# Routing attention and feed-forward on one core: clusters chosen through VectorE's 32x32 block transposes, softmax sums taken over two halves, centroids loaded first

## The chip, the core and the metric

The kernel runs on one core of a Trainium2 chip. The core has a matrix engine (TensorE, PE in the profile; its weight loads are listed as PEld), a vector engine (VectorE, DVE), a scalar engine (ScalarE, ACT), GpSimd (POOL) and SyncE (SP), which issues most of the DMA transfers. The engines run side by side and wait for one another through semaphores. TensorE writes its results to a small memory called PSUM; everything else lies in SBUF. The metric is the time of one execution on the device, in microseconds (us).

## What is computed

Two stages follow each other. The first is attention in which a query sees only the keys of its own cluster; the second is a two-layer feed-forward block with a layer norm ahead of it and a residual.

```python
# q, k, v: 4 batches x 8 heads x 768 tokens x 64, float32; 16 centroids per head
q_assign = argmax(einsum('bhsd,hcd->bhsc', q_n, c_n))    # rows normalised
k_assign = argmax(einsum('bhsd,hcd->bhsc', k_n, c_n))
scores = scale * q @ k^T, and -1e9 where q_assign != k_assign
attn = exp(scores - max) / (sum(exp(scores - max)) + 1e-9)
x = attn @ v                                             # heads side by side: 4 x 768 x 512
xn = (x - mean) / sqrt(var + 1e-6) * g_ln
out = x + relu(xn @ w_ch1) @ w_ch2                       # 512 -> 2048 -> 512
```

The length of a query or key doesn't change which centroid is nearest, so the kernel normalises only the centroids.

## The kernel before

**Tiling.** Two heads make a pair; 4 batches of 4 pairs give 16 pairs, numbered n. The 768 tokens are six tiles of 128 (`NT`), or two halves of 384 (`HC`, index g). For a pair, q and k lie transposed in SBUF (`t0`, `t1`): the 64 features of the first head (j = 0) in partitions 0 to 63, of the second in 64 to 127. A score tile has 128 keys as partitions and 384 queries as columns, one for each head.

**The loop.** The order of PE, DVE and ACT is written out by hand. Each pair has two slots, one for each half g of the queries. In a slot TensorE computes six score tiles for each head (`scores`), some smaller products, and then weighs the values with the exponentials (`weigh`, 24 matmul records). Each score tile is the sum of two products: one of bfloat16 mask tiles, which adds a huge negative number where the clusters differ, and one of k and q. ScalarE then takes the exponential (L391) into `e`. Score tiles have three buffers, so that TensorE can be a few ahead of ScalarE. After the weighing ScalarE copies the result to `x` (L422).

**Choosing clusters for pair n+1 while pair n is at work.** In slot 0 `prep_transpose` turns k and q on VectorE (L278) and `prep_sims` multiplies them with the centroids (L300). Its result has four groups of 32 rows: queries and keys of the first half, queries and keys of the second; in each, 16 clusters of one head and 16 of the other. ScalarE copies it to SBUF (L309), `prep_turn` transposes it on TensorE in three pieces (L316), after the weighing of slot 0, and `prep_route` lets VectorE find the greatest of each 16 (L325) and mark it with a one (L327). In slot 1, between the scores and the weighing, `prep_onehot` transposes the marks back on TensorE in six pieces (L342), and ScalarE writes the masks in three instructions (L363): `m` over all 128 partitions, and two strips of 16 partitions of `mask`. For the first pair the strips are written by VectorE (L365).

**Softmax sums.** VectorE adds the six exponential tiles of a half (`add_up`): L439 and L442 add them in twos, leaving two partial sums side by side, and L444 adds these to one tile, `es`. In slot 0 of the next pair `finish(n, 0)` multiplies `es` with a matrix of ones (L456, four matmuls, each into a strip of 32 partitions of one bank), and ScalarE copies the sums out (L464). The bank is shared with `weigh`, which has to wait for that copy. The last pair adds its tiles one after another (L432).

**Start.** `load(0, "q")`, the centroids and `load(0, "k")` are issued on SP in this order (half of q and k on ACT). `norm_centroids` normalises the centroids on VectorE with one square root on ScalarE, `turn_centroids` transposes them, and `busy` runs filler matmuls. The first pair's q and k are transposed on TensorE (L283). VectorE also converts the feed-forward weights in the loop (L246 to L266). The feed-forward stage, from about 339 us on, isn't touched.

Of the kernel before, what the change touches and what calls it, by code (L numbers as in the profile page):

```python
# [19 lines left out]
def kernel(  # L20
# [94 lines left out]
                    )  # L115
            loaded[n][name] = t

    load(0, "q")

    c_sb = const.tile([H * NCL, D], F32, name="c_sb")  # L120
    nc.sync.dma_start(out=c_sb, in_=centroids.rearrange("h c d -> (h c) d"))
    load(0, "k")

    ident = const.tile([P, P], F32, name="ident")
    make_identity(nc, ident)
    identb = const.tile([P, P], BF16, name="identb")
    nc.gpsimd.tensor_copy(identb, ident)
# [12 lines left out]
    onehot = route.tile([P, TH, NHALF, 2, 2, Q], BF16, name="onehot")  # L140
    nc.gpsimd.memset(onehot, 0.0)
    NG = TH * NHALF * 2 * 2

    mask = heads.tile([P, S], BF16, name="mask", bufs=1)
    nc.gpsimd.memset(mask, 0.0)
    hits = const.tile([P, B * NPAIR], F32, name="hits")
    far = const.tile([P, 2], F32, name="far")
    for rows, bias, scale in ((slice(0, D), 0.0, 1.0), (slice(D, P), -FAR, FAR)):  # L150
        nc.gpsimd.memset(far[rows, 0:1], bias)
        nc.gpsimd.memset(far[rows, 1:2], scale)

    DE = HC // Q
    rdens = const.tile([P, B * NPAIR, DE], F32, name="rdens")
# [137 lines left out]
    def prep_sims(n):  # L293

        _, pr = pairs[n]
        sim = ps("sim_ps")
        for side in range(2):
            for g in range(NHALF):
                r = (g * 2 + side) * Q
                nc.tensor.matmul(  # L300
                    sim[r : r + Q, :HC],
                    cT[:, pr, :, :].rearrange("p j c -> p (j c)"),
                    prepared[n][side][:, g * HC : (g + 1) * HC],
                    start=True,
                    stop=True,
                    tile_position=(0, r),
                )
        sim_sb = route.tile([P, HC], F32, tag="sim", name="sim_sb")
        nc.scalar.copy(sim_sb, sim[:, :HC])  # L309
        prepared[n]["sim"] = sim_sb  # L310

    def prep_turn(n):
        sim_sb = prepared[n]["sim"]
        simT = ps("simT_ps")
        for c in range(TH):
            nc.tensor.transpose(  # L316
                simT[:, c * P : (c + 1) * P], sim_sb[:, c * P : (c + 1) * P], ident
            )
        prepared[n]["simT"] = simT

    def prep_route(n):
        simT = prepared[n]["simT"]
        sims = simT[:, :HC].rearrange("p (g c) -> p g c", c=NCL)
        best = route.tile([P, NG], F32, tag="best", name="best")
        nc.vector.tensor_reduce(best, sims, AX.X, ALU.max)  # L325

        nc.vector.scalar_tensor_tensor(  # L327
            out=onehot.rearrange("p c g s j d -> p (c g s j) d")[:, :, :NCL],
            in0=sims,
            scalar=1.0,  # L330
            in1=best.unsqueeze(2).to_broadcast([P, NG, NCL]),
            op0=ALU.mult,
            op1=ALU.is_equal,
            accum_out=hits[:, n : n + 1],
        )

    def prep_onehot(n):
        t = ps("oh_ps", BF16, 1024)
        for g in range(NHALF):
            for c in range(TH):  # L340
                o = (g * TH + c) * P
                nc.tensor.transpose(  # L342
                    t[:, o : o + P],
                    onehot[:, c, g, :, :, :].rearrange("p s j d -> p (s j d)"),
                    identb,
                )

        m = heads.tile([P, S], BF16, tag="m", name="m", bufs=1)
        shade(n, m, t[:, :S], slice(0, P))
        z = mask  # L350
        prepared[n]["oh"] = t
        prepared[n]["m"] = [(z[:D], m[:D]), (m[D:], z[D:])]

    def prep_mask(n, j):
        t, z = prepared[n]["oh"], mask
        src, dst = ((D, 0), (Q, D + Q))[j]
        src, dst = slice(src, src + NCL), slice(dst, dst + NCL)
        shade(n, z[dst], t[src, :S], src)

    def shade(n, out, src, rows):  # L360
        add, factor = far[rows, 0:1], far[rows, 1:2]
        if n or rows == slice(0, P):
            nc.scalar.activation(out, src, AF.Identity, bias=add, scale=factor)  # L363
        else:
            nc.vector.tensor_scalar(out, src, factor, add, op0=ALU.mult, op1=ALU.add)  # L365

# [11 lines left out]
    def scores(i, first="mask", parts=("mask", "qk", "exp")):  # L378
        n, g, c = steps[i]
        st = prepared[n]  # L380
        if parts[0] == first:
            st["s", i] = ps_s.tile([P, 2, 512], F32, tag="s", name="s_ps")
        s = st["s", i]
        keys, cols = slice(c * P, (c + 1) * P), slice(g * HC, (g + 1) * HC)
        rows = [slice(j * D, (j + 1) * D) for j in range(2)]
        for part in parts:
            if part == "exp":
                if c % 2 == 0:
                    soft[i // 2] = attn.tile([P, 2, 2, HC], F32, tag="e", name="e", bufs=4)
                e = soft[i // 2][:, c % 2]  # L390
                nc.scalar.activation(e, s[:, :, :HC], AF.Exp, scale=SCALE)  # L391
                continue
            for j in range(2):
                of_keys, of_queries = st["m"][j] if part == "mask" else [st[i][rows[j]] for i in (1, 0)]
                nc.tensor.matmul(  # L395
                    s[:, j, :HC], of_keys[:, keys], of_queries[:, cols],
                    start=part == first, stop=part != first, skip_group_check=True,
                )

# [25 lines left out]
    def add_up(n, g, parts=range(2)):  # L425
        u = (n * NHALF + g) * NT // 2
        if n + 1 == len(pairs):

            es = xpool.tile([P, 2, HC], F32, tag="row", name="es", bufs=2)
            e = [two[:, h] for two in [soft.pop(u + m) for m in range(NT // 2)] for h in range(2)]  # L430
            for m in range(1, NT):
                nc.vector.tensor_tensor(es, e[0] if m == 1 else es, e[m], ALU.add)  # L432
            sums[n, g] = es
            return
        if 0 in parts:
            two = xpool.tile([P, 3, S], F32, tag="sums", name="two", bufs=2)
            two = two[:, :2].rearrange("p h (j c) -> p h j c", j=2)
            sums[n, g] = two
            nc.vector.tensor_tensor(two, soft.pop(u), soft.pop(u + 1), ALU.add)  # L439
        if 1 in parts:  # L440
            two = sums[n, g]
            nc.vector.tensor_tensor(two, two, soft.pop(u + 2), ALU.add)  # L442
            es = last.tile([P, 2, HC], F32, tag="es", name="es", bufs=3)
            nc.vector.tensor_tensor(es, two[:, 0], two[:, 1], ALU.add)  # L444
            sums[n, g] = es

    def finish(n, part):
        b, pr = pairs[n]  # L450
        if part == 0:
            den = ps_a.tile([P, 512], F32, tag="a", name="den_ps") if n + 1 < len(pairs) else ps("den_ps")
            for j in range(2):
                for g in range(NHALF):
                    r = (j * NHALF + g) * Q
                    nc.tensor.matmul(  # L456
                        den[r : r + Q, :HC], ones, sums[n, g][:, j, :],
                        start=True, stop=True, tile_position=(0, r),
                    )
# [178 lines left out]
    for n in range(len(pairs) - 1):  # L638
        for slot in (0, 1) if n < TWICE else (0,):
            convert[n, slot] = len(convert)  # L640
    order = {mybir.EngineType.PE, mybir.EngineType.DVE, mybir.EngineType.Activation}
    limit[0] = len(convert)
    with tc.manual_schedule(engines=order | {mybir.EngineType.SP}):
# [6 lines left out]

        busy(26)
        norm_centroids(0)
        prep_transpose(0, 0)
        load(1, "q")
        load(0, "v")
        norm_centroids(1)
        norm_centroids(2)
        busy(4)
        prep_transpose(0, 1)
        load(1, "k")  # L660
        busy(8)
        turn_centroids()
        busy(8)
        nc.scalar.activation(warm, warm, AF.Exp, scale=0.0)
        prep_sims(0)
        busy(10)
        prep_turn(0)
        scores(0, "qk", ("qk",))
        prep_route(0)
        prep_onehot(0)  # L670
        prep_mask(0, 0)
        prep_mask(0, 1)
        for i in range(1, AHEAD):
            scores(i, "qk", ("qk",))
        for i in range(AHEAD):
            scores(i, "qk", ("mask", "exp"))
# [2 lines left out]
    with tc.manual_schedule(engines=order | {mybir.EngineType.Pool}):  # L679
        for u in range(len(pairs) * slots):  # L680
# [12 lines left out]
            if slot == 0:  # L693
                if n and nxt:
                    finish(n - 1, 0)
                if nxt:
                    prep_sims(n + 1)
            elif nxt:
                prep_onehot(n + 1)
                prep_mask(n + 1, 0)  # L700
                prep_mask(n + 1, 1)
            for job in extra.pop((n, f"between {slot}"), ()):
                job()
            if slot and n > 1 and nxt:
# [15 lines left out]
            if slot == 0:  # L720
                load(n + 1, "v")
                if nxt:
                    prep_turn(n + 1)
                    prep_route(n + 1)
                else:
                    for part in (2, 3):
# [479 lines left out]
```

## Time and profile before

Three runs took 925.67, 925.93 and 926.99 us; the median is 925.93.

| | |
|---|---|
| profiled execution | 926.89 us |
| span of its instructions | 925.0 us |
| until the first weighing starts | 19.4 us |
| the attention loop, to the first feed-forward matmul | 319.2 us |
| feed-forward | 586.4 us |
| busy in the loop: PE, DVE, ACT | 317.5, 292.4, 225.1 us |

The profile lists groups of instructions by line, engine, operation and tiles: how often, the busy time in all, the mean length of one in nanoseconds, and the idle time of the engine just ahead of them with what ended it. Records of TensorE overlap, since matmuls are pipelined: a record's length is not what it adds to the time, and the distance from one start to the next is read from the timeline.

```profile
L316 PE MATMUL simT_ps<-ident,sim_sb 128*128 128x128 f32 x48 | 8.7, 291 | 0.0
L342 PE MATMUL oh_ps<-identb,onehot 128*128 128x128 bf16 x96 | 8.1, 221 | 0.4 <-DVE onehot L327 0.4
...
L444 DVE TENSOR_TENSOR es<-two 128x768 f32<-128x768 f32 x30 | 28.7, 958 | 1.0
```

"128x128 f32" is the shape of the moving operand, x48 the count of records, "8.7, 291" the busy microseconds of the group and the mean nanoseconds of one record.

### The profile page before, as it was taken

What the parts mean: (1) busy time and instruction counts of PE and PEld (TensorE: products, weight loads), DVE (VectorE), ACT (ScalarE), POOL (GpSimd) and SP (SyncE); (2) the same over time, 40 slices, a digit from 0 to 9 for tenths busy, and PEclk for the clock granted to TensorE, in tenths of its full rate; (3) what the DMA queues carried; (4) which work ended last, traced back from release to release, by engine and by line L of the source; (5) the groups of instructions that cost most, each with busy time, mean ns of one, the idle gap of its engine ahead of it and who ended that gap; (6) DMA issues with size and microseconds to landing.
All of it is one profiled execution on the core that took longest, in us unless ns stands there. A gap on an engine that the chain in (4) does not pass through costs nothing.

```text
span 925.0 us, 12294 instructions
## 1 busy us (share of the span) xinstructions
PE 913.7 (99%) x4634; PEld 584.9 (63%) x4634; DVE 610.4 (66%) x1050; ACT 346.1 (37%) x545; POOL 77.7 (8%) x145
## 2 busy tenths in 40 slices
PE   8999999999999999999999999999999999999997
PEld 4444444444444445568885558886557887557886
DVE  5989999998899879989763446362446372435331
ACT  4677677668777743330003330002331001332000
POOL 1112222111112111110000000000000000000000
PEclk9999999999999999999999999999999999999999
DMA  7778889998796346645530002120002021000011
GB/s 161 145 167 164 162 166 193 212 189 172 164 197 134 83 90 162 141 114 167 164 105 6 0 1 97 54 75 14 0 1 86 29 92 34 1 1 11 26 46 37
DMA packets 186578, 89.32 MB, mean 97 GB/s; under 512 B 153632, under 2 KB 170128, under 8 KB 186512
## 3 DMA queue, kind: packets, MB, share of 16 engines
q1 hardware_dynamic: 177200, 73.09, 33.5%
q0 software_dynamic: 7712, 14.99, 8.2%
q8 instruction: 38, 0.62, 0.3%
q10 hardware_dynamic: 1600, 0.39, 0.2%
q14 instruction: 28, 0.23, 0.1%
HBM read 62.52 MB, written 17.52 MB: 87 GB/s over the span
## 4 chain that ended last, share of the span: by engine, by line
PE 98%; ACT 0%; DMA 0%; DVE 0%; issue 0%; SPq 0%; ACTq 0%; DVEq 0%
PE x_ps L867 18%; PE x_ps L774 18%; PE s_ps L395 17%; PE a_ps L407 14%; PE z_ps L867 9%; PE z_ps L774 9%; PE y_ps L867 4%; PE y_ps L774 4%; PE den_ps L456 1%; PE sim_ps L300 1%; PE simT_ps L316 1%; PE oh_ps L342 1%; DMA k_sb<-in_k_dram 0%; ACT e L391 0%; DVE mask L365 0%
## 5 line engine op out<-in xcount | busy, mean ns | idle before, releaser
L391 ACT ACTIVATE e<-s_ps 128x768 f32<-128x768 f32 x192 | 152.5, 812 | 23.2 <-PE s_ps L395 20.2
L395 PE MATMUL s_ps<-t,t 64*128 64x384 f32 x768 | 155.1, 483 | 0.0
L407 PE MATMUL a_ps<-e,v_sb 128*64 128x384 f32 x768 | 130.9, 490 | 0.0
L407 PEld LDWEIGHTS a_ps<-e,v_sb 128*64 128x64 f32 x768 | 52.3, 137 | 69.6 <-issue 58.3
L794 DVE TENSOR_TENSOR h<-z_ps,u 128x384 f32<-128x384 f32 x64 | 35.6, 556 | 91.2 <-PE z_ps L774 68.7
L395 PEld LDWEIGHTS s_ps<-t,t 64*128 64x128 f32 x768 | 68.1, 188 | 35.0 <-issue 34.4
L867 PE MATMUL x_ps<-w2t,h 128*128 128x256 f32 x384 | 84.5, 379 | 0.0
L802 ACT ACTIVATE h<-h 128x384 f32<-128x384 f32 x96 | 49.5, 522 | 85.6 <-DVE h L794 85.6
L867 PEld LDWEIGHTS x_ps<-w2t,h 128*128 128x128 f32 x384 | 72.7, 190 | 10.1
L395 PE MATMUL s_ps<-m,mask 64*128 64x384 bf16 x192 | 62.1, 324 | 1.6 <-ACT e L391 1.2
L395 PE MATMUL s_ps<-mask,m 64*128 64x384 bf16 x192 | 61.9, 324 | 0.4 <-DVE mask L365 0.4
L439 DVE TENSOR_TENSOR two<-e 128x1536 f32<-128x1536 f32 x30 | 52.6, 1753 | 11.7 <-ACT e L391 11.7
L789 ACT COPY u<-x_ps 128x384 f32<-128x384 f32 x64 | 30.6, 479 | 75.1 <-PE x_ps L774 75.1
L442 DVE TENSOR_TENSOR two<-two,e 128x1536 f32<-128x1536 f32 x30 | 52.6, 1754 | 1.7
L878 DVE TENSOR_TENSOR o_sb<-x_ps,xb 128x256 f32<-128x256 f32 x48 | 20.1, 418 | 49.1 <-PE x_ps L867 49.1
L789 ACT COPY p<-x_ps 128x384 f32<-128x384 f32 x32 | 15.0, 468 | 96.3 <-PE x_ps L774 96.3
L774 PE MATMUL x_ps<-xn,w 128*128 128x384 f32 x128 | 46.6, 487 | 0.6 <-ACT late L422 0.6
L774 PE MATMUL x_ps<-xt,ws 128*128 128x384 f32 x128 | 46.6, 487 | 0.0
L774 PE MATMUL z_ps<-xt,ws 128*128 128x384 f32 x128 | 46.5, 486 | 0.0
L774 PE MATMUL x_ps<-xn,ws 128*128 128x384 f32 x128 | 46.5, 486 | 0.0
L774 PE MATMUL y_ps<-xn,w 128*128 128x384 f32 x128 | 46.5, 486 | 0.0
L774 PE MATMUL x_ps<-xt,w 128*128 128x384 f32 x128 | 46.5, 486 | 0.0
(146 smaller groups left out, 1395.6 us busy)
## 6 DMA issues: line engine op xcount, KB each, us to landing
raw<-in_moe_w_ch_dram SPq DMA_DIRECT2D x32, 512.0 KB, 5.3
w<-tb POOLq DMA_DIRECT2D x32, 256.0 KB, 5.7
v_sb<-in_v_dram SPq DMA_DIRECT2D x32, 192.0 KB, 5.6
xr<-x_d SPq DMA_DIRECT2D x24, 256.0 KB, 3.4
xb<-x_d SPq DMA_DIRECT2D x48, 128.0 KB, 2.2
out_dram<-o_sb SPq DMA_DIRECT2D x48, 128.0 KB, 1.7
q_sb<-in_q_dram SPq DMA_DIRECT2D x62, 96.0 KB, 3.5
k_sb<-in_k_dram SPq DMA_DIRECT2D x62, 96.0 KB, 5.4
```

The source lines that it names most:

```text
L300: nc.tensor.matmul(sim[r : r + Q, :HC], cT[:, pr, :, :].rearrange("p j c -> p (j c)"), prepared[n][side][:, g * HC : (g + 1) * HC], start= ...
L391: nc.scalar.activation(e, s[:, :, :HC], AF.Exp, scale=SCALE)
L395: nc.tensor.matmul(s[:, j, :HC], of_keys[:, keys], of_queries[:, cols], start=part == first, stop=part != first, skip_group_check=True,)
L407: nc.tensor.matmul(acc[j * D : (j + 1) * D, :HC], loaded[n]["v"][:, j, c, :], e[:, j, :], start=(c == 0), stop=(c == NT - 1),)
L439: nc.vector.tensor_tensor(two, soft.pop(u), soft.pop(u + 1), ALU.add)
L442: nc.vector.tensor_tensor(two, two, soft.pop(u + 2), ALU.add)
L774: nc.tensor.matmul(bank[:, :HC], lhs[:, c, :], rhs[:, c, :], start=first and c == 0, stop=c == NDH - 1, skip_group_check=True,)
L789: nc.scalar.copy(t, bank[:, :HC])
L794: nc.vector.tensor_tensor(h, bank[:, :HC], other, ALU.add)
L802: nc.scalar.activation(h, h, AF.Relu)
L867: nc.tensor.matmul(bank[:, :MH], hidden[lhs + (c,)][:, tt * P : (tt + 1) * P], rhs[:, c, :], start=first and c == 0, stop=c == NFH - 1, sk ...
L878: nc.vector.tensor_tensor(o, bank[:, :MH], x, ALU.add)
```

## The change

The similarities are transposed in blocks of 32x32 by VectorE, straight from PSUM, and so are the marks. Because every block stays within its 32 partitions, the marks come back in the row order of the similarities: queries and keys, each with both heads' clusters in one strip of 32 rows. The masks are therefore two tiles, one for queries and one for keys, written in seven pieces; a column of zeros and ones (`of_head`) clears the other head's clusters from the query masks. Six pieces are written in slot 1 of pair n for pair n+1, the seventh, which only the second half of the queries uses, in slot 0 of that pair. `prep_turn`, `prep_onehot` and the copy of the similarities are gone.

The partial sums of the exponentials are no longer added to one tile; `finish` multiplies both with ones and lets TensorE add them in PSUM.

At the start the centroids are loaded ahead of q, their square root is taken ahead of the copies of q, they are transposed ahead of k, and fewer fillers run. The scores of the first three tiles (without mask) follow the choice of clusters in the written order.

```diff
-    load(0, "q")
 
     c_sb = const.tile([H * NCL, D], F32, name="c_sb")
     nc.sync.dma_start(out=c_sb, in_=centroids.rearrange("h c d -> (h c) d"))
-    load(0, "k")
+    load(0, "qk")
...
+    of_head = const.tile([P, 2, 2], F32, name="of_head")
+
+    def heads_own():
+        for i, starts in enumerate(((0, D + NCL), (NCL, D))):
+            for m, o in enumerate(starts):
+                nc.vector.tensor_reduce(of_head[:, i, m : m + 1], ident[:, o : o + NCL], AX.X, ALU.add)
+            nc.vector.tensor_tensor(of_head[:, i, 0:1], of_head[:, i, 0:1], of_head[:, i, 1:2], ALU.add)
...
-        sim_sb = route.tile([P, HC], F32, tag="sim", name="sim_sb")
-        nc.scalar.copy(sim_sb, sim[:, :HC])
-        prepared[n]["sim"] = sim_sb
-
-    def prep_turn(n):
...
     def prep_route(n):
-        simT = prepared[n]["simT"]
-        sims = simT[:, :HC].rearrange("p (g c) -> p g c", c=NCL)
+
+        sim = route.tile([P, HC], F32, tag="sim", name="sim_sb")
+        nc.vector.transpose(sim, prepared[n]["sim"][:, :HC])
+        sims = sim.rearrange("p (g c) -> p g c", c=NCL)
...
-    def prep_onehot(n):
...
+        oh = route.tile([P, HC], BF16, tag="oh", name="oh")
+        nc.vector.transpose(oh, onehot)
+        prepared[n]["oh"] = oh
+
+
+    def prep_mask(n, side, j, g):
+        oh = prepared[n]["oh"]
+        if side:
+            src, dst = slice((g * 2 + 1) * Q, (g * 2 + 2) * Q), slice(j * D, j * D + Q)
+            out, add, factor = mask[1][dst, g * HC : (g + 1) * HC], far[src, :], FAR
+        elif j == g:
+
+            src = slice(0, P)
+            out, add, factor = mask[0][:, :HC], 0.0, of_head[:, 0, 0:1]
         else:
...
+            src, dst = slice(g * D, g * D + Q), slice(j * D, j * D + Q)
+            out, add, factor = mask[0][dst, HC:], 0.0, of_head[src, 1, 0:1]
+        if n or side:
+            nc.scalar.activation(out, oh[src, :], AF.Identity, bias=add, scale=factor)
+        else:
+            nc.vector.tensor_scalar_mul(out, oh[src, :], factor)
...
             two = sums[n, g]
             nc.vector.tensor_tensor(two, two, soft.pop(u + 2), ALU.add)
-            es = last.tile([P, 2, HC], F32, tag="es", name="es", bufs=3)
-            nc.vector.tensor_tensor(es, two[:, 0], two[:, 1], ALU.add)
-            sums[n, g] = es
+            sums[n, g] = [two[:, h] for h in range(2)]
...
+            parts = len(sums[n, 0])
+            for h in range(parts):
+                for j in range(2):
+                    for g in range(NHALF):
+                        r = (j * NHALF + g) * Q
+                        nc.tensor.matmul(
+                            den[r : r + Q, :HC], ones, sums[n, g][h][:, j, :],
+                            start=h == 0, stop=h == parts - 1, tile_position=(0, r),
+                            skip_group_check=True,
+                        )
...
+    pieces = [(0, 0, 0), (1, 0, 0), (1, 1, 0), (0, 1, 0), (1, 0, 1), (1, 1, 1), (0, 0, 1)]
...
         norm_centroids(0)
+        norm_centroids(1)
         prep_transpose(0, 0)
         load(1, "q")
         load(0, "v")
-        norm_centroids(1)
         norm_centroids(2)
-        busy(4)
+        turn_centroids()
         prep_transpose(0, 1)
         load(1, "k")
-        busy(8)
-        turn_centroids()
-        busy(8)
+        busy(6)
+        prep_sims(0)
         nc.scalar.activation(warm, warm, AF.Exp, scale=0.0)
-        prep_sims(0)
         busy(10)
-        prep_turn(0)
-        scores(0, "qk", ("qk",))
+        heads_own()
         prep_route(0)
-        prep_onehot(0)
-        prep_mask(0, 0)
-        prep_mask(0, 1)
-        for i in range(1, AHEAD):
+        for piece in pieces:
+            prep_mask(0, *piece)
+        for i in range(AHEAD):
             scores(i, "qk", ("qk",))
...
             if slot == 0:
                 if n and nxt:
                     finish(n - 1, 0)
+                if n:
+                    prep_mask(n, *pieces[-1])
                 if nxt:
                     prep_sims(n + 1)
             elif nxt:
-                prep_onehot(n + 1)
-                prep_mask(n + 1, 0)
-                prep_mask(n + 1, 1)
+                for piece in pieces[:-1]:
+                    prep_mask(n + 1, *piece)
...
-                    prep_turn(n + 1)
                     prep_route(n + 1)
```

More of the change, by code (lines that the diff above doesn't have):

```diff
@@ L116, in load @@
             loaded[n][name] = t
-    load(0, "q")
     c_sb = const.tile([H * NCL, D], F32, name="c_sb")
     nc.sync.dma_start(out=c_sb, in_=centroids.rearrange("h c d -> (h c) d"))
-    load(0, "k")
+    load(0, "qk")
     ident = const.tile([P, P], F32, name="ident")
     make_identity(nc, ident)
-    identb = const.tile([P, P], BF16, name="identb")
-    nc.gpsimd.tensor_copy(identb, ident)
     once = attn.tile([P, 2, 2, HC], F32, tag="e", name="once", bufs=4)[:, 0]
@@ L138 @@
     nc.gpsimd.memset(eps, 1e-6)
[L140 to L147, printed above, removed]
-    hits = const.tile([P, B * NPAIR], F32, name="hits")
[L149 to L152, printed above, removed]
+    NG = HC // Q * 2
+    mask = [heads.tile([P, S], BF16, name=f"mask_{i}", bufs=1) for i in range(2)]
+    for m in mask:
+        nc.gpsimd.memset(m, 0.0)
+    hits = const.tile([P, B * NPAIR], F32, name="hits")
+    far = const.tile([P, 1], F32, name="far")
+    nc.gpsimd.memset(far, -FAR)
+    of_head = const.tile([P, 2, 2], F32, name="of_head")
[4 more added lines that the diff above has]
+            nc.vector.tensor_tensor(of_head[:, i, 0:1], of_head[:, i, 0:1], of_head[:, i, 1:2], ALU.add)
     DE = HC // Q
@@ L307, in prep_sims @@
                 )
-        sim_sb = route.tile([P, HC], F32, tag="sim", name="sim_sb")
-        nc.scalar.copy(sim_sb, sim[:, :HC])
-        prepared[n]["sim"] = sim_sb
-    def prep_turn(n):
[L313 to L319, printed above, removed]
+        prepared[n]["sim"] = sim
     def prep_route(n):
-        simT = prepared[n]["simT"]
-        sims = simT[:, :HC].rearrange("p (g c) -> p g c", c=NCL)
+        sim = route.tile([P, HC], F32, tag="sim", name="sim_sb")
+        nc.vector.transpose(sim, prepared[n]["sim"][:, :HC])
+        sims = sim.rearrange("p (g c) -> p g c", c=NCL)
         best = route.tile([P, NG], F32, tag="best", name="best")
         nc.vector.tensor_reduce(best, sims, AX.X, ALU.max)
+        onehot = route.tile([P, HC], BF16, tag="onehot", name="onehot")
         nc.vector.scalar_tensor_tensor(
-            out=onehot.rearrange("p c g s j d -> p (c g s j) d")[:, :, :NCL],
+            out=onehot.rearrange("p (g c) -> p g c", c=NCL),
             in0=sims,
@@ L335, in prep_route @@
         )
-    def prep_onehot(n):
[L338 to L363, printed above, removed]
-        else:
-            nc.vector.tensor_scalar(out, src, factor, add, op0=ALU.mult, op1=ALU.add)
+        oh = route.tile([P, HC], BF16, tag="oh", name="oh")
[9 more added lines that the diff above has]
+            out, add, factor = mask[0][:, :HC], 0.0, of_head[:, 0, 0:1]
+        else:
+            src, dst = slice(g * D, g * D + Q), slice(j * D, j * D + Q)
[4 more added lines that the diff above has]
+            nc.vector.tensor_scalar_mul(out, oh[src, :], factor)
     xT_d = [spill.tile([NDC, P, S], F32, name=f"xT_d{b}") for b in range(B)]
@@ L383, in scores @@
         s = st["s", i]
-        keys, cols = slice(c * P, (c + 1) * P), slice(g * HC, (g + 1) * HC)
+        keys = slice(c * P, (c + 1) * P)
         rows = [slice(j * D, (j + 1) * D) for j in range(2)]
@@ L393, in scores @@
             for j in range(2):
-                of_keys, of_queries = st["m"][j] if part == "mask" else [st[i][rows[j]] for i in (1, 0)]
+                of_queries, of_keys = [(mask if part == "mask" else st)[i][rows[j]] for i in range(2)]
+                o = (g ^ j if part == "mask" else g) * HC
                 nc.tensor.matmul(
-                    s[:, j, :HC], of_keys[:, keys], of_queries[:, cols],
+                    s[:, j, :HC], of_keys[:, keys], of_queries[:, o : o + HC],
                     start=part == first, stop=part != first, skip_group_check=True,
@@ L432, in add_up @@
                 nc.vector.tensor_tensor(es, e[0] if m == 1 else es, e[m], ALU.add)
-            sums[n, g] = es
+            sums[n, g] = [es]
             return
         if 0 in parts:
-            two = xpool.tile([P, 3, S], F32, tag="sums", name="two", bufs=2)
-            two = two[:, :2].rearrange("p h (j c) -> p h j c", j=2)
+            if g == 0:
+                two = xpool.tile([P, 3, S], F32, tag="sums", name="two", bufs=2)[:, :2]
+            else:
+                two = last.tile([P, 2, S], F32, tag="two", name="two", bufs=1)
+            two = two.rearrange("p h (j c) -> p h j c", j=2)
             sums[n, g] = two
@@ L442, in add_up @@
             nc.vector.tensor_tensor(two, two, soft.pop(u + 2), ALU.add)
-            es = last.tile([P, 2, HC], F32, tag="es", name="es", bufs=3)
-            nc.vector.tensor_tensor(es, two[:, 0], two[:, 1], ALU.add)
-            sums[n, g] = es
+            sums[n, g] = [two[:, h] for h in range(2)]
     def finish(n, part):
@@ L452, in finish @@
             den = ps_a.tile([P, 512], F32, tag="a", name="den_ps") if n + 1 < len(pairs) else ps("den_ps")
[L453 to L459, printed above, removed]
+            parts = len(sums[n, 0])
[8 more added lines that the diff above has]
+                        )
             if n + 1 < len(pairs):
```

## The prediction

> **What bounds the kernel now.** I read the page first (engine totals, granted clock, chain that ended last), then the PE groups by shape, then the timeline of one pair of heads, then the waits.
>
> ```profile
> span 925.0 us, 12294 instructions
> PE 913.7 (99%) x4634; PEld 584.9 (63%) x4634; DVE 610.4 (66%) x1050; ACT 346.1 (37%) x545; POOL 77.7 (8%) x145
> ...
> PEclk9999999999999999999999999999999999999999
> ...
> PE 98%; ACT 0%; DMA 0%; DVE 0%; issue 0%; SPq 0%; ACTq 0%; DVEq 0%
> ```
>
> TensorE is busy 99%, its clock is full, and 98% of the chain runs through it: time moves only by what TensorE executes or waits for. VectorE and ScalarE count only where TensorE comes to wait for them. A busy PE hides small waits, so I took start-to-start distances from the timeline, here of the fifth pair:
>
> ```profile
> 99.18 0.85 PE L456 MATMUL den_ps<-es,ones 128*32 128x384 f32 x8
> ...
> 99.85 0.83 PE L300 MATMUL sim_ps<-t,cT 128*32 128x384 f32 x8
> ...
> 100.63 4.09 PE L407 MATMUL a_ps<-e,v_sb 128*64 128x384 f32 x24
> ...
> 104.65 0.55 PE L316 MATMUL simT_ps<-ident,sim_sb 128*128 128x128 f32 x3
> ...
> 105.13 0.33 PE L395 MATMUL s_ps<-m,mask 64*128 64x384 bf16 x1
> ```
>
> From start to next start: sums (den) 0.67, similarities 0.78, weighing 4.02, first transposes 0.48. The scores then take 4.95 (105.13 to 110.08), the second transposes 0.44 (110.08 to 110.52), weighing 4.02 (to 114.54), the next pair's scores 4.95. A pair takes 20.31 us, the same in nearly every pair: TensorE never waits in the loop for more than it hides.
>
> ```profile
> 110.08 0.51 PE L342 MATMUL oh_ps<-identb,onehot 128*128 128x128 bf16 x6
> 110.52 0.20 PEld L407 LDWEIGHTS a_ps<-e,v_sb 128*64 128x64 f32 x4
> 110.52 4.09 PE L407 MATMUL a_ps<-e,v_sb 128*64 128x384 f32 x24
> ...
> 111.04 0.99 ACT L363 ACTIVATE m<-oh_ps,far 128x768 bf16<-128x768 bf16 x1
> ...
> 112.04 1.99 ACT L363 ACTIVATE mask<-oh_ps,far 16x768 bf16<-16x768 bf16 x2
> ...
> 114.54 0.33 PE L395 MATMUL s_ps<-m,mask 64*128 64x384 bf16 x1
> ...
> 114.66 0.48 ACT L422 COPY x<-a_ps 128x384 f32<-128x384 f32 x1 [0.63 <-PE a_ps L407]
> ```
>
> Here is the one close race: the masks are ready at 114.03, the next scores start at 114.54.
>
> **TensorE transposes go.** Per pair 3 (L316) and 6 (L342) leave. Without them the neighbours meet directly, at no extra price: weighing to scores takes 4.02 at the pair's end as it does to the transposes, and scores to weighing takes 4.95 in the last pair (320.04 to 324.99), which has none. Fifteen pairs pass through the loop: 15 x (0.48 + 0.44) = 13.8 us. The Trainium skill, VectorE: DVE Perf Modes, "The three transpose paths", prices one 128x128 transpose on TensorE at 390 ns. By that, 9 x 0.39 x 15 = 52.7 us would go; the rows have 0.16 and 0.07 apiece, because they stream. The row decides.
>
> **Softmax sums double.** L456 reads two halves in place of one: 4 more matmuls (8 records) in each of 15 pairs; the last keeps one. The 8 records now take 0.67 before the next in the same tiling; the second half accumulates on the first, as L407 does back to back. 15 x 0.67 = 10.05 us added. Bounds: 0.60, and 1.0 if each strip had to wait out its own first pass (a record lasts 0.498, so 0.33 more). I take 0.67.
>
> The copy of the sums (L464) then starts 0.67 later, at 1.59 after the first sum, and ends at 2.07; weighing, which needs that bank, would start at 0.67 + 0.67 + 0.78 = 2.12. The two were tied before and stay tied.
>
> **VectorE.** Gone: two adds of 958 ns (L444) per pair. New: two 128x384 transposes, each about half of L278's 128x768 (935 to 973), 0.49 each. Some 0.9 us per pair is saved, 14 us in all, worth nothing by itself: nothing on PE waits for it. Is the choice of clusters late? Its chain grows by 1.0, but starts 0.96 earlier (the add ahead of it is gone), and its reader moves from PE at 110.08 to ACT at 111.04. So not. Holding both halves longer costs nothing: the second tile is rewritten some 10 us after its sums are taken.
>
> **ScalarE, the added wait.** Three mask writes of 0.98 to 0.99 (L363) become six of 128x384 or 32x384 here and one in the other half of the pair, where the 0.48 copy of the similarities goes. Nearest rows:
>
> ```profile
> L802 ACT ACTIVATE h<-h 128x384 f32<-128x384 f32 x96 | 49.5, 522 | 85.6 <-DVE h L794 85.6
> L363 ACT ACTIVATE mask<-oh_ps,far 16x768 bf16<-16x768 bf16 x30 | 29.5, 984 | 0.6
> L830 ACT ACTIVATE h<-x_ps 128x384 f32<-128x384 f32 x32 | 15.7, 492 | 29.0 <-PE x_ps L774 26.8
> ```
>
> Width costs (812 - 479) / 384 = 0.87 ns an element (L391 against L422), so L363 at 384 wide is 984 - 333 = 651. It has two per-partition operands, the new ones have one; L545 against L175 (299, 206; six elements wide) puts one at about 89. Reading SBUF costs 30 (L802 against L830). So 651 - 89 + 30 = 592, say 0.60; ends 0.52 (L802) and 0.68 (both operands).
>
> Count from the weighing's start, now right after the scores: the exponentials end at 0.93, six pieces with gaps of 0.02 at 4.65, then the copy of x (L422), queued behind them, at 5.15. Scores start at 4.02 and need only four pieces (3.41); the two for later keys are first used 2.4 us later. The exponentials queued behind want 4.02 + 1.04; they begin at 5.17, 0.11 late, and the three score buffers allow about 0.5. **No stall**, until a piece costs over 0.665; at 0.68 it is 6 x 0.70 - 4.11 = 0.1 per pair, 1.5 us. At one place it shows: after pair 15 of 16 the sums wait for that copy (ACT x, 0.58), weighing to sums 4.67 now, 5.17 then: +0.5 us.
>
> **Start.** Centroids go ahead of q on SP (0.49 of issue). Their chain starts at
>
> ```profile
> 4.88 0.23 DVE L170 TENSOR_TENSOR once<-c_sb 128x64 f32<-128x64 f32 x1 [3.92 <-DMA c_sb<-in_centroids_dram]
> ...
> 8.51 0.85 PE L300 MATMUL sim_ps<-t,cT 128*32 128x384 f32 x8 [0.26 <-DVE cT L195]
> ...
> 15.20 4.33 ACT L391 ACTIVATE e<-s_ps 128x768 f32<-128x768 f32 x6 [1.82 <-PE s_ps L395]
> 15.85 0.98 DVE L278 STREAM_TRANSPOSE t<-k_sb 128x768 f32<-128x768 f32 x1 [1.06 <-DMA k_sb<-in_k_dram]
> ```
>
> and would start a microsecond sooner. Similarities then wait for the copies of k (7.76): 7.85, not 8.51. VectorE's chain (transpose 0.5, maximum 0.56, compare 0.64, transpose 0.5) ends near 11.1; three small products stay on VectorE, four pieces on ScalarE end near 13.5: the first exponential is 1.7 us earlier. Little survives. Pair 1's k and q follow on SP after q's own transposes, which shift by 0 to 0.45; they land near 16.2, are transposed in 0.98 + 0.93, and the next similarities start near 18.2 instead of 18.59. I take -0.4 (ends -1.5 and +0.4). The six small operations that mark a head's rows fit before 8.7. Fewer filler matmuls (42 for 56): the Trainium skill, TensorE: Matmul & The Clock Gate, Part 1, says that an idle window of about 3.4 us halves the clock, which speaks against removing them. The row has full clock in every slice and I see no such gap; were it so, a couple of microseconds of matmuls would double there, mostly behind the landing of k.
>
> **Sum.** -13.8 + 10.05 + 0.5 - 0.4 = -3.65 us. The profiled execution took 926.89, of it 925.0 span; the median of runs is 925.93, 0.96 below. The difference carries over: 925.93 - 3.65 = **922.3 us**.
>
> **Rivals.**
> - *ScalarE becomes the bound at the pair's end* (slower). Place: the six pieces, with x's copy and the exponentials behind. For: L363's time hardly depends on rows (991 for 128, 984 for 16), so narrow pieces are not cheap. Against: half the width. It cancels the gain at 0.71 a piece; at 0.80 it stalls 6 x 0.82 - 4.11 = 0.81 a pair, 12.2 us: 934.
> - *The second half of the sums is dear* (1.0 us): 5 us more, 927 at that end, 925 to 926 midway. Against: four strips run side by side now, and L407 accumulates without waiting.
> - *The choice fails to come out unique* and the general path runs: the time would be far beyond these. The comparison still covers 24 groups of 16 clusters. 1%.
>
> **Chances.** Forecast 0.79, within 920.3 to 924; dear sums 0.12; ScalarE's stall 0.08; general path 0.01. About 0.2% (1.9 us) is what a measurement here can tell from no change. Faster 0.80, same 0.11, slower 0.09. Range 920.2 to 925.0: its top takes in a piece of 0.68, the start's bad end and a third of the dear sums' case.
>
> **What would show it.** No L316 or L342; 16 records of den taking 1.34 to the next start; weighing to scores 4.02 at both places; a pair near 20.06; seven mask writes near 0.60, the first exponential near 13.5, the second similarities near 18.2. A PE wait on ScalarE at a pair's end, or a longer pair, would make it wrong.

## The result and the profile after

The changed kernel took 922.31 us (median of four runs, 921.64 to 923.32), against 926.2 for the kernel before beside it (925.67 to 926.99): a ratio of 0.9958, 95% interval 0.9941 to 0.9975. The gain of 3.9 us is small but clear of zero.

The page of the changed kernel: span and engine totals, granted clock of TensorE, and the shares of the chain that ended last.

```profile
span 920.4 us, 12283 instructions
...
PE 908.6 (99%) x4596; PEld 578.0 (63%) x4596; DVE 600.0 (65%) x1059; ACT 357.5 (39%) x592; POOL 77.8 (8%) x141
...
PEclk9999999999999999999999999999999999999999
...
PE 65%; ACT 0%; DVE 0%; issue 0%
```

TensorE is as full as before, 5.1 us shorter in busy time, at full clock. VectorE lost 10.4 us, ScalarE gained 11.4. The chain was followed back over only 65% of the span this time, so it says nothing of the loop; the stages have to be read from the timeline.

| profiled execution | before | after | difference |
|---|---|---|---|
| whole execution, us | 926.89 | 922.19 | -4.70 |
| its span | 925.03 | 920.35 | -4.68 |
| until the first weighing | 19.37 | 18.07 | -1.30 |
| loop, to the first feed-forward matmul | 319.26 | 315.85 | -3.41 |
| feed-forward | 586.40 | 586.43 | +0.03 |

In the loop, the timeline of the fifth pair, for TensorE and ScalarE (start, length, engine, line, output and operands, records joined in the row):

```profile
96.14 1.50 PE L445 MATMUL den_ps<-two,ones 128*32 128x384 f32 x16
97.46 0.83 PE L302 MATMUL sim_ps<-t,cT 128*32 128x384 f32 x8
98.24 4.09 PE L393 MATMUL a_ps<-e,v_sb 128*64 128x384 f32 x24
102.27 0.34 PE L381 MATMUL s_ps<-mask,mask 64*128 64x384 bf16 x2
...
107.21 4.09 PE L393 MATMUL a_ps<-e,v_sb 128*64 128x384 f32 x24
108.17 0.61 ACT L348 ACTIVATE mask<-oh,of_head 128x384 bf16<-128x384 bf16 x1
108.80 1.25 ACT L348 ACTIVATE mask<-oh,far 32x384 bf16<-32x384 bf16 x2
110.07 0.61 ACT L348 ACTIVATE mask<-oh,of_head 32x384 bf16<-32x384 bf16 x1
110.71 1.25 ACT L348 ACTIVATE mask<-oh,far 32x384 bf16<-32x384 bf16 x2
111.24 0.34 PE L381 MATMUL s_ps<-mask,mask 64*128 64x384 bf16 x2
111.98 0.48 ACT L408 COPY x<-a_ps 128x384 f32<-128x384 f32 x1
112.36 0.82 ACT L376 ACTIVATE e<-s_ps 128x768 f32<-128x768 f32 x1
```

Read the starts. The 16 records of the sums take 1.31 to the similarities (the 8 records took 0.67), similarities 0.78 as before, weighing to scores 4.02 in both slots (98.24 to 102.27, 107.21 to 111.24), and scores to weighing 4.95 with no transpose between. From one pair's sums to the next is 20.04, against 20.31. ScalarE's six pieces follow one another from 108.17 on, right behind the exponentials; the next scores begin at 111.24 while the last two pieces are still being written, and the copy of `x` and the exponentials follow without TensorE waiting for them.

The start, from the timeline (in brackets: idle time of the engine ahead of it, and what ended it):

```profile
2.75 0.22 DVE L172 TENSOR_TENSOR once<-c_sb 128x64 f32<-128x64 f32 x1 [1.80 <-DMA c_sb<-in_centroids_dram]
...
7.24 1.14 PE L302 MATMUL sim_ps<-t,cT 128*32 128x384 f32 x8
...
13.44 4.33 ACT L376 ACTIVATE e<-s_ps 128x768 f32<-128x768 f32 x6
...
15.39 0.98 DVE L280 STREAM_TRANSPOSE t<-k_sb 128x768 f32<-128x768 f32 x1 [3.56 <-DMA k_sb<-in_k_dram]
...
17.29 0.85 PE L302 MATMUL sim_ps<-t,cT 128*32 128x384 f32 x8 [0.38 <-DVE t L280]
```

The first exponential is 1.76 earlier than before (15.20). The second similarities are 1.30 earlier (18.59), and the first weighing behind them is 1.30 earlier too. What ends the wait now is the arrival of the second pair's k: VectorE sat idle for 3.56 us until it came.

### The profile page after: what moved, and what is told of

The parts are those of the page before. It is cut to its first block, busy times and chain, and to the rows that moved or that the text cites. A ratio compares the mean times of both kernels' runs of the same rounds, so it can differ in the third digit from the quotient of the medians.

```text
span 920.4 us, 12283 instructions
## 1 busy us (share of the span) xinstructions
PE 908.6 (99%) x4596; PEld 578.0 (63%) x4596; DVE 600.0 (65%) x1059; ACT 357.5 (39%) x592; POOL 77.8 (8%) x141
## 4 chain that ended last, share of the span: by engine, by line
PE 65%; ACT 0%; DVE 0%; issue 0%
PE x_ps L855 18%; PE x_ps L762 18%; PE z_ps L855 9%; PE z_ps L762 9%; PE y_ps L855 5%; PE y_ps L762 4%; PE s_ps L381 1%; PE a_ps L393 1%; PE den_ps L445 0%; ACT late L408 0%; DVE o_sb L878 0%; PE stat_ps L545 0%; PE flag_ps L737 0%
## 5 line engine op out<-in xcount | busy, mean ns | idle before, releaser
L381 PE MATMUL s_ps<-mask,mask 64*128 64x384 bf16 x384 | 63.0, 324 | 2.8 <-ACT e L376 2.1
L381 PEld LDWEIGHTS <-mask 64*128 64x128 bf16 x384 | 19.2, 94 | 43.9 <-issue 13.2
```

What stands on the lines that cost most here:

```text
L381: nc.tensor.matmul(s[:, j, :HC], of_keys[:, keys], of_queries[:, o : o + HC], start=part == first, stop=part != first, skip_group_check=True,)
```

## Experiments

Each theory and its rivals are quoted as they stood before the runs. All experiments start from the changed kernel, except the first.

### The sums alone

The kernel before, with nothing changed but the sums: no third add, both halves multiplied with ones. The partial sums of a pair's second half get a tile of their own, and `finish` is as in the change; neither is shown here.

```diff
-            es = last.tile([P, 2, HC], F32, tag="es", name="es", bufs=3)
-            nc.vector.tensor_tensor(es, two[:, 0], two[:, 1], ALU.add)
-            sums[n, g] = es
+            sums[n, g] = [two[:, h] for h in range(2)]
...
```

> The kernel before with one part of the change alone: the softmax sums read both halves, the third add is gone; transposes stay on TensorE, start as before. Theory (TensorE is the bound, each second half costs it 0.645 us in 15 pairs): 926.2 + 9.7 = 935.9 us, pair of heads 20.96 us. Rival (the gain of the change comes from VectorE's relief): not slower than before, 926 us or less.

It took 936.68 us (936.27 to 936.78) against 926.54: ratio 1.0108, 1.0091 to 1.0125. The timeline of its fifth pair:

```profile
101.12 1.50 PE L459 MATMUL den_ps<-two,ones 128*32 128x384 f32 x16
102.44 0.83 PE L300 MATMUL sim_ps<-t,cT 128*32 128x384 f32 x8
```

Again 1.31 between the starts, 0.64 more than before, and a pair takes 20.96: 15 x 0.645 = 9.7 us of TensorE time, and the loop is longer by just that (328.96 against 319.26). This rules out the dear second half (1.0) and shows that this part of the change alone makes the kernel slower.

### The third add back on VectorE

If the sums cost 9.7 us, why not keep the third add? The changed kernel with it:

```diff
-            sums[n, g] = [two[:, h] for h in range(2)]
+            es = last.tile([P, 2, HC], F32, tag="es", name="es", bufs=3)
+            nc.vector.tensor_tensor(es, two[:, 0], two[:, 1], ALU.add)
+            sums[n, g] = es
...
```

The tiles of the partial sums and `finish` are those of the kernel before again.

> The changed kernel with VectorE's third add back, so that TensorE reads one tile of sums again: the transposes part and the new start without the sums part. If TensorE stays the bound: 922.3 - 9.7 = 912.6 us, pair 19.40 us. My theory is that VectorE takes over: in the changed kernel it is busy 17.6 to 19.4 us of each pair's 20.04, with the adds 19.5 to 21.3 against TensorE's 19.40; so 917 to 925 us, pairs of 20 to 21 us while weights are converted twice a pair (the first seven) and near 19.6 after, with TensorE waits that VectorE ends.

It took 925.34 us (924.09 to 925.95, ten runs): ratio 0.9986, 0.9977 to 0.9996. That is 3.0 us slower than the change, where TensorE's work alone would have given 912.6. The timeline of its fifth pair shows what stood in the way:

```profile
94.63 0.96 DVE L430 TENSOR_TENSOR es<-two 128x768 f32<-128x768 f32 x1
...
96.57 0.85 PE L442 MATMUL den_ps<-es,ones 128*32 128x384 f32 x8
...
97.30 0.97 DVE L280 STREAM_TRANSPOSE t<-k_sb 128x768 f32<-128x768 f32 x1
98.19 0.94 DVE L280 STREAM_TRANSPOSE t<-q_sb 128x768 f32<-128x768 f32 x1
...
99.18 0.85 PE L302 MATMUL sim_ps<-t,cT 128*32 128x384 f32 x8 [1.76 <-DVE t L280]
```

The sums cost little again, but the similarities come 2.61 after them, not 0.67, because VectorE turns k and q too late. From 98 to 118 us VectorE is busy 19.44 of 20 us (in the changed kernel 18.44). In the kernel before it was already busy 19.70 of the 20.30 us of the fifth pair, so there was next to no room for two transposes and a shorter pair. From sums to sums, five pairs in the middle take 21.34 to 21.36; from the sums of the twelfth pair on a pair takes 19.40, with VectorE keeping up. So the block transposes use the room that the third add left: the two parts of the change belong together, but only in the first two thirds of the loop.

### One and two more pieces for ScalarE

The prediction put ScalarE's stall at 0.71 a piece. Writing the last piece once or twice more prices it.

```diff
-                for piece in pieces[:-1]:
+                for piece in pieces[:-1] + pieces[-2:-1] * 1:
                     prep_mask(n + 1, *piece)
```

> The changed kernel with one mask piece written twice in each pair's second slot (same values). Theory (ScalarE's queue at the pair's end has about 0.4 us left before TensorE waits; a piece takes 0.637 with its gap): 0.2 us of stall in each of 15 pairs and 0.64 at the last pair's sums, 926 us. Rival (ScalarE is hidden by far): 922.3 us, pair 20.04.

> As the run before, with two pieces more. Theory: 0.84 us of stall a pair and 1.3 at the last, 922.3 + 13.9 = 936 us. Rival (hidden): 922.3 us.

One more: 925.39 us, ratio 0.9992 (0.9982 to 1.0001). Two more: 936.01, ratio 1.0102 (1.0086 to 1.0119). The timeline of the run with one more piece:

```profile
92.26 0.34 PE L381 MATMUL s_ps<-mask,mask 64*128 64x384 bf16 x2
...
93.65 0.48 ACT L408 COPY x<-a_ps 128x384 f32<-128x384 f32 x1
...
94.02 4.33 ACT L376 ACTIVATE e<-s_ps 128x768 f32<-128x768 f32 x6
...
94.89 0.34 PE L381 MATMUL s_ps<-mask,mask 64*128 64x384 bf16 x2
```

The exponentials begin 1.76 after the scores' start; the fourth score tile, which needs the first tile's buffer, starts 1.0 after the third (93.89; 0.81 otherwise). The scores then take 5.16, not 4.95: 0.21 a pair with one piece more, and 0.85 with two. A piece costs 0.64 with its gap, so the change keeps 0.43 in hand, and ScalarE holds back nothing until it is spent. At the last pair's sums the wait for the copy of `x` is 1.80 with one piece more, and the clock stays full; with two it grows to 2.44, and behind it the clock falls. Windows view (stretch, length, then busy time and records of PE, PEld, DVE, ACT, POOL, then granted clock, DMA share, GB/s):

```profile
327.90:331.20 3.30, 3.30 (x16) 1.60 (x14) 0.00 (x0) 1.29 (x2) 0.62 (x2) 0.50 0.01 2
```

The scores behind that wait take 6.41, not 4.95. The working for two more pieces had no such loss, so part of its agreement with 936.01 is luck.

### The third add on GpSimd

```diff
+            nc.gpsimd.tensor_tensor(es, two[:, 0], two[:, 1], ALU.add)
+            sums[n, g] = [es]
```

In the written order the second half of `finish` moves behind the turn's additions, so that the add doesn't queue on GpSimd behind the transfer that `finish` issues there.

> The changed kernel with the third add on GpSimd in all pairs but the last. If it disturbs nothing, TensorE's bound alone: 922.3 - 9.7 = 912.6 us, pair 19.40. Rival: GpSimd is late for the sums, or slows VectorE while both run: TensorE waits at the sums or at the similarities, 916 us or more. No row shows an add on GpSimd, so neither is preferred by much.

It took 941.56 us, ratio 1.0162 (1.0147 to 1.0178): the rival's direction, far beyond the 916 that it named. Groups by shape (busy us and mean ns behind the bar):

```profile
L433 POOL TENSOR_TENSOR es<-two 128x768 f32<-128x768 f32 x30 | 60.9, 2029 | 95.9 <-DVE rdens L463 71.0 <-DVE two L431 24.7
L267 DVE TENSOR_SCALAR tb<-w 128x512 uint32<-128x512 uint32 x32 | 29.2, 912 | 1.0
```

The add takes 2029 ns there (958 on VectorE), and VectorE's L267, 426 ns in the changed kernel, takes 912 on the mean. VectorE has the same work as in the changed kernel, and is busy for 636.2 us, not 600.0. By the waits of its matmuls TensorE sits idle for 14.4 us until VectorE has turned k and q and for 3.4 us until an add is done, and from 104.5 to 111.2 and from 329.7 to 336.5 its granted clock was 0.50. The Trainium skill, SBUF — State Buffer, "Who interferes with whom", has GpSimd and VectorE share a pair of ports that one instruction holds to its end, and names `tensor_scalar` among those that can want it. The doubled row fits that. No run here separated it from other causes, nor the add from the moved half of `finish`.

### The third add where VectorE has room

The second experiment says that from the twelfth pair's sums on VectorE keeps up. So the add comes back for pairs n >= 9 only. In the last turn but one, the sixth piece of the masks is also written behind the copy of `x`, which the last pair's sums wait for.

```diff
-            sums[n, g] = [two[:, h] for h in range(2)]
+            if n < 9:
+                sums[n, g] = [two[:, h] for h in range(2)]
+            else:
+                es = last.tile([P, 2, HC], F32, tag="es", name="es", bufs=2)
+                nc.vector.tensor_tensor(es, two[:, 0], two[:, 1], ALU.add)
+                sums[n, g] = [es]
...
-                for piece in pieces[:-1]:
+                for piece in pieces[: 5 if n + 2 == len(pairs) else 6]:
...
+            if slot and n + 2 == len(pairs):
+                prep_mask(n + 1, *pieces[5])
```

> The changed kernel, but pairs 9 to 14 (counted from 0) get VectorE's third add back, and pair 14 writes its last mask piece behind the copy of x. Theory (VectorE has room for the adds once weights are converted only once a pair and the norm rows are done; TensorE is the bound): six second halves go, 6 x 0.645 = 3.9 us, and the wait for the copy of x at the last pair, 0.6: 922.3 - 4.5 = 917.8 us, pairs 20.04 before and 19.40 after. Rival (VectorE is the bound in those pairs too, as in the first ones): 922 us or more, with sums starting late by VectorE.

919.05 us (918.85 to 919.22), ratio 0.9922 (0.9909 to 0.9936): faster than both kernels. Its late pairs take 19.42, and with the moved piece weighing to sums takes 4.67 at the last pair, not 5.25. It is 1.25 us above the 917.8 worked out: this profile's first weighing came at 18.62 (18.07 in the change), and in the last pair the timeline shows a new wait:

```profile
310.76 0.83 PE L450 MATMUL den_ps<-es,ones 128*32 128x384 f32 x2 [0.58 <-ACT x L408]
312.00 0.85 PE L450 MATMUL den_ps<-es,ones 128*32 128x384 f32 x6 [0.41 <-DVE es L436]
312.78 0.34 PE L381 MATMUL s_ps<-mask,mask 64*128 64x384 bf16 x2
```

The first two records run, the other six wait for the second half's add: 2.02 from sums to scores, where two halves without an add would take about 1.4. So pair 14 keeps the halves (`if n < 9 or n + 2 == len(pairs)`):

> As the run with the third add in late pairs, but pair 14 keeps both halves, so that its sums don't wait for VectorE's add (2.02 us from the sums to the scores there, 1.43 in the changed kernel). Theory: 919.05 - 0.6 = 918.5 us, weighing to sums 4.67 and sums to scores 1.43 at the last pair. Rival (something else than the add holds the last pair's start): 919 us, 2.0 stays.

Its timeline at the same place:

```profile
310.41 0.48 ACT L408 COPY x<-a_ps 128x384 f32<-128x384 f32 x1
...
310.94 1.50 PE L450 MATMUL den_ps<-two,ones 128*32 128x384 f32 x16 [0.58 <-ACT x L408]
```

The scores start at 312.37, 1.43 after the sums, and the loop takes 312.14, against 312.75. The median, 918.93 (917.83 to 920.74; ratio 0.9924, 0.991 to 0.9937), can't be told from 919.05: the start alone varies by as much. So the timeline bears the theory out, and the medians decide nothing here. Both are more than 7 us faster than the kernel before.

### The start

Three versions of the start ask what its part is worth: the start of before (q, centroids, k; its order of steps and fillers, but the first scores placed as in the change) with the new choice of clusters; the change with q loaded ahead of the centroids, k behind; and that with fillers in the hole.

```diff
@@ q ahead, in both of the latter @@
+    load(0, "q")
     c_sb = const.tile([H * NCL, D], F32, name="c_sb")
...
-    load(0, "qk")
+    load(0, "k")
@@ with more fillers, besides @@
+        busy(26)
         turn_centroids()
...
-        busy(6)
+        busy(20)
         prep_sims(0)
```

> The changed kernel with the start of before: q ahead of the centroids, 30 fillers ahead of k, the centroids turned after k. Theory (the new start ends at the landing of pair 1's k, the old one at the chain of the choice): the choice by VectorE still helps the old start, first weighing near 18.8 where the change has 18.07 and before 19.37; 923.0 us. Rival (the order of the start does nothing, all came from VectorE's shorter chain): first weighing 18.1, 922.3 us.

> The changed kernel with q loaded ahead of the centroids and nothing else undone. The centroids land near 4.9 in place of 2.75, TensorE comes to k only behind them: similarities near 8.7 for 7.24, first weighing near 19.0, 923.2 us. Rival (the load order doesn't matter, since k's landing decides): first weighing near 18.1, 922.3 us.

> The changed kernel with q ahead of the centroids, as in the earlier run, and with fillers: 26 while TensorE waits for the centroids and 20 for 6 ahead of the similarities. Theory (that run lost most of its 3.7 us at the start to a halved clock in two stretches, since TensorE was idle; the load order alone costs under 1): full clock from about 5 us on, similarities near 8.6, first weighing near 18.8, 923 us. Rival (the load order is the loss): first weighing near 21.7 again.

The start of before: 923.5 us (921.99 to 923.73; ratio 0.9968, 0.9955 to 0.9981), first weighing at 18.72, as worked out (18.8). q ahead: 923.8 (ratio 0.9975, 0.9966 to 0.9985), but in its trace the first weighing came at 21.73, not 19.0. That execution, at 925.25, is one of the two longest of ten. Its windows, columns as above:

```profile
5.50:7.00 1.50, 0.01 (x1) 0.01 (x1) 1.03 (x6) 0.95 (x3) 0.00 (x0) 1.00 0.26 41
7.00:10.40 3.40, 3.40 (x21) 2.18 (x21) 1.62 (x9) 1.68 (x2) 0.00 (x0) 0.51 0.83 155
10.40:17.20 6.80, 4.55 (x36) 2.40 (x34) 4.92 (x10) 4.07 (x8) 0.00 (x0) 0.99 0.92 232
17.20:20.70 3.50, 3.50 (x16) 1.75 (x12) 3.36 (x5) 2.44 (x4) 0.00 (x0) 0.52 0.48 90
```

TensorE had nothing from 5.2 to 7.0, waiting for the centroids, and then ran at half clock for 3.4 us; it happened again at 17.2, after a thin stretch. With fillers in the hole, the same view:

```profile
5.50:7.00 1.50, 1.21 (x23) 1.04 (x20) 1.00 (x6) 0.95 (x3) 0.00 (x0) 1.00 0.24 39
7.00:10.40 3.40, 3.40 (x45) 2.57 (x45) 2.05 (x10) 1.96 (x3) 0.00 (x0) 1.00 0.87 164
...
17.20:20.70 3.50, 3.50 (x28) 1.43 (x26) 3.43 (x6) 2.12 (x4) 0.00 (x0) 1.00 0.73 180
```

Full clock, and the first weighing at 19.17: most of the 2.6 us between these two executions was the clock, not the order of loads. The median is no better for it, 924.69 (ratio 0.9978, 0.9969 to 0.9987), because its executions fall in two groups: three of 922.6 to 922.9 with a mean granted clock of 0.999, the profiled one among them, and eight of 923.5 to 925.4 with 0.996 or 0.997. One stretch of 3.4 us at half clock takes 0.0018 off the mean (1.7 of 920), so the longer executions may have one such stretch each. That isn't shown: only one execution is profiled, and the mean also takes in the end of the span, where TensorE has no work left (in the change's profile the clock is 0.50 from 917.0 to 920.4, and the mean 0.998 from that alone). The three medians lie too close to say which order of loads is best.

## Why the prediction was right, step by step

The kernel was predicted at 922.3 with a change of -3.65; the medians moved by -3.9. The loop came out through its terms; the start was mis-sized by 0.6. With the start's mean of seven profiles (below) the terms would make -4.4, so that the sum lies so near to -3.9 is in part luck; the interval of the ratio, -5.5 to -2.3 us, holds both.

| step | predicted | measured |
|---|---|---|
| transposes on TensorE gone, neighbours meet directly | -13.8; 4.02 and 4.95 | all 144 records gone; 4.02 and 4.95 |
| second half of the sums, each of 15 pairs | +0.67 | +0.645 (1.31 for 16 records) |
| from pair to pair | 20.06 | 20.04 |
| last pair, weighing to sums | 4.67 to 5.17 | 4.67 to 5.25 |
| until the first weighing | -0.4 | -1.30 in the profile |

**TensorE.** The loop's -3.41 is the predicted -13.8 + 10.05 + 0.5 = -3.25 with a slightly cheaper sum (15 x 0.025 = 0.4 less) and 0.08 more of a wait in the last pair: -3.5. The transposes were worth their distance in the stream, 0.48 and 0.44 a pair. By an estimate from the Trainium skill's price (VectorE: DVE Perf Modes, "The three transpose paths"), 390 ns for one in bfloat16, the loop would have lost some 39 us more than it did. The rival of the dear sums is ruled out by the 1.31, here and in the first experiment, and nothing in the times points to the general path.

**ScalarE.** 0.60 was predicted for a piece. Groups by shape:

```profile
L348 ACT ACTIVATE mask<-oh,far 32x384 bf16<-32x384 bf16 x64 | 39.1, 612 | 3.2 <-DVE oh L331 1.9
L348 ACT ACTIVATE mask<-oh,of_head 128x384 bf16<-128x384 bf16 x15 | 9.2, 615 | 0.4
...
L331 DVE STREAM_TRANSPOSE oh<-onehot 128x384 bf16<-128x384 bf16 x16 | 9.3, 578 | 1.5
L315 DVE STREAM_TRANSPOSE sim_sb<-sim_ps 128x384 f32<-128x384 f32 x16 | 9.2, 576 | 0.6 <-PE sim_ps L302 0.6
```

A piece takes 612 to 615 over 32 partitions and over 128. The exponentials start 0.08 later than otherwise (0.11 predicted), no tile of scores waits, and the runs with more pieces give the stall at the place and size that the working gave. The rival that ScalarE becomes the bound had the mechanism right, and the change is one piece away from it: one more makes TensorE wait 0.21 a pair, two make it slower than the kernel before.

The one wait that does show is in the last pair. The timeline of the changed kernel:

```profile
313.37 0.48 ACT L408 COPY x<-a_ps 128x384 f32<-128x384 f32 x1
...
313.90 1.50 PE L445 MATMUL den_ps<-two,ones 128*32 128x384 f32 x16 [1.16 <-ACT x L408]
```

The wait for the copy of `x` doubled, from 0.58 to 1.16.

**VectorE.** Its transposes were put at 0.49 and take 0.58, since a transpose doesn't halve with its width (973 for 768 columns, 576 for 384). The relief is 0.76 a pair, not 0.9. "Worth nothing by itself" holds: in the first experiment the relief alone gave nothing back. The second adds what the prediction left out: without it the new transposes make VectorE the bound in the early pairs.

**Where the prediction failed: the start.** "Little survives" was the wrong step. It had pair 1's k land "near 16.2", by shifting the old arrival later with the later issue. It was issued later (9.96, not 9.35), but the transfers took 3.2 to 3.4 us from issue to landing, not 3.4 to 4.0, and k was being transposed at 15.39. Before, the first weighing came at 19.37 or 19.38 in both profiles with the old start and the old choice, set by the chain that chooses the clusters; now a landing mostly sets it, and it varies. The seven profiles that keep the change's order of loads and steps at the start have it at 17.64 to 18.82, 18.36 on the mean. So the term is -1.0, with 0.5 to 0.7 to either side, rather than -0.4; -1.3 was this one execution.

The experiments part it as far as single profiles can. With the old order of loads and steps, the new choice of clusters brings the first weighing to 18.72, with no wait for k ahead of the similarities: 0.65 from the chain. The new order shortens the chain by 1.1 more (first exponential at 13.44 for 14.55), and in the one profile where k came early enough, that of the third add back on VectorE, the first weighing came at 17.64. On the mean the landing takes 0.7 of these 1.1 back; the 0.4 that is left is less than the scatter.

One agreement at the start is luck: the first exponential came at 13.44, as worked out (13.5), but the similarities ahead of it began at 7.24, not 7.85, and the chain between took 6.2, not 5.65.

**Fillers.** The prediction weighed the rule on idle windows (the Trainium skill, TensorE: Matmul & The Clock Gate, Part 1) and saw no gap. In the profile of the change every part of the start has full clock. The margin was thinner than the page's window of about 3.4 us suggests, though: with q ahead, a hole of 1.8 us was followed by a stretch at half clock. Holes of nearly that length stayed without one in other runs (1.76 us five times with the third add back on VectorE, 1.80 in the last pair with one more piece), so the length of one hole doesn't decide it, and what does wasn't found.

## What to carry to other kernels

On an engine that is never idle, price a removed or added instruction by the distance from start to start in its stream, and then count what is queued on each engine that takes over its work: ScalarE's 0.43 us in hand were the whole margin here. Two parts of a change may pay for one another only in some of a loop's turns: the add that VectorE had to give up early in the loop was affordable again later, and giving it back there, with one mask piece moved, brought 3.3 us more. A transfer that other work used to hide is not a fixed length; once a start waits for a landing, compare several profiles before giving a fraction of a microsecond to anything.

## What the runs showed of the hardware

- VectorE's 32x32 block transposes of 128x384 took 576 ns from PSUM in float32 and 578 from SBUF in bfloat16 (memory and type differ together, so neither is priced alone). From 973 ns for 768 columns of float32, an estimate is about 1.03 ns a column and 180 ns fixed.
- An add of two 128x768 float32 tiles took 2029 ns on GpSimd, 958 on VectorE, and beside it a 128x512 VectorE operation with one tensor operand went from 426 to 912 ns on the mean.
- TensorE's clock went to 0.50 for about 3.4 us behind idle stretches of 1.8 us (at the start, q ahead) and 2.44 us (in the last pair, two more pieces). Idle stretches of 1.76 us (five times, third add back on VectorE) and 1.80 us (in the last pair, one more piece) left it at full clock in their profiles.
